# TensorE's filler products before the first group: from full 32-bit products of 128 columns to one-pass products of 128, 256 and 512 columns

## The chip, the cores and the metric

The kernel runs on one core of a Trainium2 chip. The metric is device time in microseconds (us), the median of several runs. Its engines are TensorE (PE, with its weight loads, PEld), VectorE (DVE), ScalarE (ACT), GpSimd (POOL) and SyncE (SP, which here only issues transfers). Each runs its own list of instructions in order and waits for the others by semaphores. TensorE's clock is granted by a throttle, and the profile records it.

## The reference

A gated linear recurrence over 768 steps for 4 batches and 8 heads of 48 channels is followed by a layer with a cosine gate. Cut to what is computed:

```
a_n = a * min(|a|, 0.999) / (|a| + 1e-6)          # a = a_re + i a_im
for t in range(768):
    S = a_n[t] * S + outer(k[t], v[t])            # complex state, 48 x 48 per head
    y[t] = q[t] @ real(S)
x = y as (3072, 384)
h = x @ w_in                                      # (3072, 2048)
out = (h * cos(h)) @ w_out                        # (3072, 384)
```

## The kernel before

The 3072 rows are cut into 24 chunks of 128 steps, taken two at a time: 12 groups. For a group the kernel computes logarithms of the gates' magnitudes and their angles, sums both along time by products with triangular matrices, scales and turns keys and queries by the results, and then needs only matrix products: scores within a chunk, a state carried between chunks, and the two products of the layer.

The function concerned is `fast_path`. For the first group the order on each engine is written out by hand (lines 1225 to 1247); afterwards a helper, `weave`, spreads steps over each other by given shares. All of TensorE's work passes through `matmul` (line 683) or through the transposes of `f_turn` and `f_columns` (lines 918 and 976), each chained behind the one before it, so TensorE's order is that of the program. Since the helper records them, most TensorE instructions of the profile carry line 684, and VectorE's and ScalarE's carry 673, 699 (table load) or 703 (functions from a table): they are told apart by their tiles.

The steps of the first group that the text speaks of, in TensorE's order:

- `busy(12)` at line 1227: twelve filler products whose result is read by no one. The stationary operand is the identity `ident`, the moving one the triangular matrix `sums[0]`. Both are constants that ScalarE's queue fetches at the start (lines 572 and 573), `ident` first.
- `p_powers(0, i)` for the two chunks (line 1232): a product `lgs` of `sums[0]` with the logarithms `lg`, 384 columns; ScalarE takes two exponentials of it (`lg`, here also named `P`, and `Q`). After each, `busy(8)`.
- `g_angle`: ScalarE's arctangent over both chunks into `tan`. Then `g_phase` for each chunk: products `phs` of `turns` with `tan`, and for the second chunk a product of `last` with the first chunk's result; ScalarE rounds `phs`, VectorE subtracts.
- `g_trig`, `p_apply`, `g_stack`: sines and cosines, and the products that make the turned keys `ks` and queries `qs`. Ahead of `g_stack`, `busy(12)`.
- then `f_turn` (tile `tp`, transposes of `ks` and `qs` into `kT` and `qT`), `f_scores` (`sc`), `f_state` (`sp`), `f_rows` (`yr`), `f_columns` (`xp`) of both chunks, and the first group's layer (`hp`).

Fillers write to a buffer of the same PSUM rotation of five (`pa`, tag "a") as `lgs`, `phs`, `tp`, `sc` and the others. From the third group on, the phases and the sums of logarithms are products in the one-pass form of 32-bit floats, with an upper and a lower half of the operand (`hi`, `lo`, line 784). Weights arrive as 64-bit floats in the tile `raw` by GpSimd's queue and are put together by VectorE and ScalarE into `w_in` and `w_out` (line 619).

Of the kernel before, what the change touches and what calls it, by code (L numbers as in the profile page):

```python
# [11 lines left out]
F32 = mybir.dt.float32  # L12
# [3 lines left out]
F32R = mybir.dt.float32r  # L16
# [471 lines left out]
def fast_path(ctx, tc, q, k, v, a_re, a_im, moe_w_in, moe_w_out, out, least, odd, wide):  # L488
# [6 lines left out]
    nc = tc.nc  # L495
    B, H, S, D = q.shape
    DM, DF = moe_w_in.shape
    C = 128
# [21 lines left out]
    stage = {"pool": room.enter_context(tc.tile_pool(name="stage", bufs=1)), "bufs": 4}  # L520
    pa = ctx.enter_context(tc.tile_pool(name="pa", bufs=5, space=PSUM))
# [11 lines left out]
    def constant(array, name, queue=nc.scalar, pool=consts):  # L533
        t = pool.tile(list(array.shape), F32, name=name)
        queue.dma_start(out=t, in_=nc.inline_tensor(array, name=name + "_const").ap())
        return t

    def scalar_tile(value, name):
        t = consts.tile([C, 1], F32, name=name)
        nc.vector.memset(t, value)  # L540
        return t
# [30 lines left out]
    ident = constant(np.eye(C, dtype=np.float32), "ident", pool=stage["pool"])  # L572
    sums = [constant(sums_np[0], "sums", pool=stage["pool"])]
# [61 lines left out]
                          accum_out=odd[:, ds(next(odds), 1)])  # L635

    nc.vector.memset(odd, 0.0)
    odds = iter(range(odd.shape[1]))
    carrier_b = scalar_tile(2.0 ** 23, "carrier_b")
    least_e_b = scalar_tile(897.0, "least_e_b")  # L640
# [8 lines left out]
    def chain(ins, engine="scalar"):  # L649

        if engine in tail:
            behind(ins, tail[engine])
        tail[engine] = ins
# [29 lines left out]
    def matmul(out, **kw):  # L683
        chain(nc.tensor.matmul(out, **kw), "tensor")  # L684

    def busy(count):

        ps = pa.tile([C, C], F32, tag="a", name="busy")
        for _ in range(count):
            matmul(ps, lhsT=ident, rhs=sums[0], start=True, stop=True)  # L690

    tables = {AF.Ln: "natural_log_exp_and_others", AF.Exp: "natural_log_exp_and_others",
              AF.Arctan: "trig_and_small", AF.Sin: "trig_and_small"}
# [2 lines left out]
    def preload(table):  # L696
        if loaded[0] != table:
            loaded[0] = table
            chain(nc.scalar.preload_act_table_set(table))  # L699
# [87 lines left out]
    def p_powers(g, i):  # L787

        x = X[g]
        if i == 0:  # L790
            x["P"], x["Q"] = x["lg"], temp("Q")
            x["row"] = rows_d.tile([G * DM], F32, tag="row", name="row")
            x["end"] = ft.tile([D2, G * H], F32, tag="end", name="end")
        ps = pa.tile([C, DM], F32, tag="a", name="lgs")
        summed_up(ps, g, i, "lg", sums[0])
        special(out=cut(x["P"], i, 1), in_=ps, func=AF.Exp)
        special(out=cut(x["Q"], i, 1), in_=ps, func=AF.Exp, scale=-1.0)
# [68 lines left out]
    def g_trig(g, i, n):  # L866
        x = X[g]
        if i == 0:
            x["cos"] = temp("rs")
            if g:  # L870
                x["sin"] = temp("lg")
        cs, sn = cut(x["cos"], i, n), cut(x["sin"], i, n)
        ph = cut(x["tan"], i, n)
        vector.tensor_scalar(out=cs.bitcast(U32), in0=ph.bitcast(U32),
                                scalar1=0x7FFFFFFF, scalar2=None, op0=ALU.bitwise_and)
        special(out=sn, in_=ph, func=AF.Sin, scale=TWO_PI)
        special(out=cs, in_=cs, func=AF.Sin, scale=-TWO_PI, bias=half_pi_b)

    def g_stack(g, i, n):
        x = X[g]  # L880
        if i == 0:
            for name in "ks", "qs":
                x[name] = gt.tile([C, G * H, 2, D], F32, tag=name, name=name)
        for name, product in ("ks", "Q"), ("qs", "mag"):
            for a, trig in enumerate(("cos", "sin")):
                vector.tensor_tensor(
                    out=x[name][:, ds(i * H, n * H), a],
                    in0=cut(x[product], i, n).rearrange("p (x d) -> p x d", d=D),
                    in1=cut(x[trig], i, n).rearrange("p (x d) -> p x d", d=D), op=ALU.mult)
# [334 lines left out]
    chain(nc.gpsimd.tensor_copy(out=exact, in_=ones), "gpsimd")  # L1224
    Ordered.by_hand = True
    preload("natural_log_exp_and_others")
    busy(12)
    one, two = (log_steps(0, i, 1) for i in range(2))
    for _ in range(5):
        next(one), next(two)  # L1230
    for i in range(2):
        p_powers(0, i)
        busy(8)
    next(one), next(two)
    g_angle(0, 0, 2)
    for i in range(2):
# [3 lines left out]
    g_trig(0, 0, 1)  # L1240
    p_apply(0, 0, 1)
    g_trig(0, 1, 1)
    busy(12)
    g_stack(0, 0, 1)
    p_apply(0, 1, 1)
    g_stack(0, 1, 1)
# [32 lines left out]
def kernel(ctx, tc, q, k, v, a_re, a_im, moe_w_in, moe_w_out, out):  # L1279
# [9 lines left out]
    odd = keep.tile([C, moe_w_in.shape[0] // C * 4 + NJ + NG + 1], F32, name="odd")  # L1289
    wide = keep.tile([C, NG * NJ // 2], F32, name="wide")  # L1290
    late = fast_path(tc, q, k, v, a_re, a_im, moe_w_in, moe_w_out, out, least, odd, wide)
    low = keep.tile([D2, 1], F32, name="low")
    nc.vector.tensor_reduce(out=low, in_=least, axis=AX.X, op=ALU.min)
# [58 lines left out]
```

## Time and profile before

| what | value |
|---|---|
| time, median of 3 runs | 676.51 us (676.01 to 678.98) |
| span of the profiled execution (no other time is given for it) | 677.3 us |
| TensorE busy / weight loads busy | 647.8 us / 580.3 us |
| VectorE / ScalarE busy | 490.3 us / 396.4 us |
| instructions | 10771 |
| mean granted TensorE clock | 0.985 |
| filler instructions on TensorE | 80 (two for each of 40 products), with 80 weight loads |

In the views, a row of instructions reads: start, duration, engine, line, operation, the written tile and the read ones, the shape of the stationary operand, the shape of the moving one, their number, and in brackets the idle time before them and what ended it. A row of stages reads: the stretch, its length, busy time and instructions of PE, PEld, DVE, ACT and POOL, the granted clock as a share of full speed, the share of the DMA engines, and GB/s.

### The profile page before, as it was taken

The numbers are of one execution on the slowest core, as the hardware profiler recorded it, in microseconds if no ns is written. First come the engines' busy times: TensorE is split into PE (matmuls) and PEld (weight loads), VectorE is DVE, ScalarE is ACT, GpSimd is POOL, SyncE is SP. The second block draws the span as 40 slices with busy tenths as digits, with TensorE's granted clock in tenths as the row PEclk, the third lists the DMA queues.
The fourth block names the chain that finished last, engine by engine and source line by source line (L and its number), as shares of the span: only waits on it lengthen the run. The fifth ranks groups of instructions, "written<-read, shape, count | busy, mean of one in ns | idle before, by whom it ended". The sixth has DMA issues, their size and how long they took to land.

```text
span 677.3 us, 10771 instructions
## 1 busy us (share of the span) xinstructions
PE 647.8 (96%) x4080; PEld 580.3 (86%) x4080; DVE 490.3 (72%) x792; ACT 396.4 (59%) x730; POOL 28.5 (4%) x47
## 2 busy tenths in 40 slices
PE   5788889999999999999999999999999999999995
PEld 5686657886799999999999999989999989999895
DVE  4879888759868778868768778868768769762251
ACT  5869775475466467367467467467367467432330
POOL 2011100000000000000000000000000000000000
PEclk8979899999999999999999999999999999999998
DMA  9778623923743864764864864854864753363000
GB/s 244 176 234 224 173 72 81 227 66 69 213 92 63 219 137 116 210 142 109 224 140 118 210 140 113 214 113 126 223 145 118 211 138 78 116 139 116 24 6 24
DMA packets 232810, 94.90 MB, mean 140 GB/s; under 512 B 208798, under 2 KB 221217, under 8 KB 232748
## 3 DMA queue, kind: packets, MB, share of 16 engines
q1 hardware_dynamic: 226252, 68.62, 44.5%
q0 software_dynamic: 5632, 25.17, 11.4%
q8 instruction: 34, 0.56, 0.4%
q10 hardware_dynamic: 864, 0.33, 0.2%
q14 instruction: 28, 0.23, 0.1%
HBM read 69.28 MB, written 24.81 MB: 139 GB/s over the span
## 4 chain that ended last, share of the span: by engine, by line
PE 79%; DVE 6%; DMA 6%; ACT 5%; issue 2%; SPq 1%; DVEq 0%; ACTq 0%
PE hp L684 32%; PE sum L684 15%; PE op L684 14%; PE yp L684 5%; PE sc L684 5%; PE sp L684 3%; PE phs L684 2%; DVE w_in L673 1%; PE lgs L684 1%; DMA raw<-in_moe_w_out_dram 1%; DMA xT<-x 1%; DMA qT<-moved 1%; DVE mag L673 1%; PE yr L684 1%; ACT L699 1%
## 5 line engine op out<-in xcount | busy, mean ns | idle before, releaser
L684 PE MATMUL hp<-xT,w_in 128*128 128x256 f32 x1152 | 254.2, 382 | 1.3 <-ACT xT L673 0.6
L684 PEld LDWEIGHTS hp<-xT,w_in 128*128 128x128 f32 x1152 | 219.9, 192 | 34.6 <-DMA xT<-x 1.9
L703 ACT ACTIVATE gate<-hp,half_pi_b 128x512 f32<-128x512 f32 x96 | 65.9, 686 | 128.0 <-PE hp L684 128.0
L673 DVE TENSOR_TENSOR gate<-hp,gate 128x512 f32<-128x512 f32 x96 | 65.5, 683 | 58.4 <-ACT junk L673 58.4
L684 PE MATMUL op<-w_out,gate 128*128 128x192 f32 (+1 forms) x448 | 103.0, 375 | 2.7 <-DVE w_out L673 2.7
L684 PEld LDWEIGHTS op<-w_out,gate 128*128 128x128 f32 x448 | 75.7, 190 | 19.7 <-DVE w_out L673 3.9
L673 ACT ACTIVATE junk<-hp 128x512 bf16<-128x512 f32 x96 | 56.5, 588 | 0.0
L684 PE MATMUL sum<-t_s,s 128*128 128x192 f32 x320 | 55.3, 326 | 0.0
L684 PEld LDWEIGHTS sum<-t_s,s 128*128 128x128 f32 x320 | 52.6, 190 | 0.0
L673 DVE TENSOR_TENSOR atm<-sc,causal 128x512 f32<-128x512 f32 x48 | 33.0, 687 | 25.4 <-PE sc L684 25.2
L684 PEld LDWEIGHTS sc<-qT,kT 96*128 96x128 f32 x384 | 47.6, 192 | 4.2 <-issue 2.2
L684 PE MATMUL sc<-qT,kT 96*128 96x128 f32 x384 | 49.4, 276 | 1.9 <-ACT qT L673 0.9
L673 ACT ACTIVATE ot<-sum 128x192 f32<-128x192 f32 x30 | 9.5, 320 | 49.4 <-PE sum L684 49.4
L699 ACT ACT_TABLE_LOAD x26 | 33.4, 1283 | 4.0 <-DMA ident<-ident_const 3.6
L673 ACT CAST tan<-phs 128x384 int32<-128x384 f32 x24 | 11.5, 479 | 39.7 <-PE phs L684 39.7
L673 DVE SCALAR_TENSOR_TENSOR ot<-op,ot 128x192 f32<-128x192 f32 x31 | 11.0, 354 | 32.3 <-ACT ot L673 23.5
L684 PE MATMUL yp<-atm,v 128*48 128x128 f32 x352 | 33.5, 277 | 0.0
L684 PEld LDWEIGHTS sp<-v,ks 128*96 128x96 f32 x320 | 29.7, 165 | 0.0
L684 PE MATMUL sp<-v,ks 128*96 128x48 f32 x320 | 29.6, 245 | 0.0
L684 PE MATMUL sum<-w_out,gate 128*128 128x192 f32 x160 | 29.6, 329 | 0.0
L684 PE MATMUL yp<-qT,state 96*48 96x128 f32 x304 | 29.6, 272 | 0.0
L684 PE MATMUL op<-t_a,gate 128*128 128x192 f32 x160 | 29.0, 332 | 0.0
(137 smaller groups left out, 992.7 us busy)
## 6 DMA issues: line engine op xcount, KB each, us to landing
moved<-tr SPq DMA_DIRECT2D x20, 768.0 KB
raw<-in_moe_w_in_dram POOLq DMA_DIRECT2D x16, 768.0 KB, 5.5
raw<-in_moe_w_out_dram POOLq DMA_DIRECT2D x16, 768.0 KB, 4.9
kT<-moved SPq DMA_DIRECT2D x40, 192.0 KB
qT<-moved SPq DMA_DIRECT2D x10, 768.0 KB
k<-in_k_dram SPq DMA_DIRECT2D x24, 192.0 KB
q<-in_q_dram SPq DMA_DIRECT2D x24, 192.0 KB
v<-in_v_dram SPq DMA_DIRECT2D x24, 192.0 KB
```

The lines of the kernel that those rows point to most:

```text
L673: ins = getattr(self.engine, op)(**kw)
L684: chain(nc.tensor.matmul(out, **kw), "tensor")
L699: chain(nc.scalar.preload_act_table_set(table))
L703: chain(nc.scalar.activation(func=func, **kw))
```

## The change

A new tile `idle`, 128 x 512 of 32-bit floats, is filled with ones by VectorE at the start. The fillers read it in place of `sums[0]`, with a given number of moving columns, and both operands are read in the one-pass form of 32-bit floats (`F32R`). The counts change: 12 of 128 columns become 20 of 256; 8 of 128 become 10 of 512 after the first `lgs` and 16 of 128 after the second; 12 of 128 become 24 of 256 ahead of `g_stack`.

```diff
@@ -635,6 +635,8 @@
     nc.vector.memset(odd, 0.0)
+    idle = stage["pool"].tile([C, 512], F32, name="idle")
+    nc.vector.memset(idle, 1.0)
     odds = iter(range(odd.shape[1]))
@@ -683,11 +685,12 @@
-    def busy(count):
+    def busy(count, width):
 
-        ps = pa.tile([C, C], F32, tag="a", name="busy")
+        ps = pa.tile([C, width], F32, tag="a", name="busy")
         for _ in range(count):
-            matmul(ps, lhsT=ident, rhs=sums[0], start=True, stop=True)
+            matmul(ps, lhsT=ident.bitcast(F32R), rhs=idle[:, 0:width].bitcast(F32R),
+                   start=True, stop=True)
@@ -1224,13 +1227,13 @@
     preload("natural_log_exp_and_others")
-    busy(12)
+    busy(20, 256)
     one, two = (log_steps(0, i, 1) for i in range(2))
     for _ in range(5):
         next(one), next(two)
     for i in range(2):
         p_powers(0, i)
-        busy(8)
+        busy((10, 16)[i], (512, 128)[i])
     next(one), next(two)
     g_angle(0, 0, 2)
@@ -1240,7 +1243,7 @@
     g_trig(0, 1, 1)
-    busy(12)
+    busy(24, 256)
     g_stack(0, 0, 1)
```

## The prediction

> **What bounds the kernel now.** I read the page first, then the instructions of TensorE over the first 75 us, then the chain of waits there, then busy time by stage with the granted clock, and last the one-pass products that the kernel already has. The page gives the whole:
>
> ```profile
> PE 647.8 (96%) x4080; PEld 580.3 (86%) x4080; DVE 490.3 (72%) x792; ACT 396.4 (59%) x730; POOL 28.5 (4%) x47
> PE   5788889999999999999999999999999999999995
> PEclk8979899999999999999999999999999999999998
> PE 79%; DVE 6%; DMA 6%; ACT 5%; issue 2%; SPq 1%; DVEq 0%; ACTq 0%
> ```
>
> TensorE sets the end: it is full from about 120 us, and nothing of the change lies there. All fillers run before 26 us, in slices where TensorE is not full. So the change counts only by how it moves the first group's chain, whose delay later work then inherits. TensorE's instructions in order of time (start, duration, tiles; times overlap by the pipeline's depth):
>
> ```profile
> 4.12 4.81 PE L684 MATMUL busy<-sums,ident 128*128 128x128 f32 x24 [4.12 <-DMA sums<-sums_const]
> 12.10 1.65 PE L684 MATMUL lgs<-lg,sums 128*128 128x384 f32 x2 [3.16 <-DVE lg L673]
> 13.54 2.61 PE L684 MATMUL busy<-sums,ident 128*128 128x128 f32 x16
> 15.99 0.81 PE L684 MATMUL lgs<-lg,sums 128*128 128x384 f32 x2
> 16.63 1.95 PE L684 MATMUL busy<-sums,ident 128*128 128x128 f32 x16
> 19.91 1.56 PE L684 MATMUL phs<-tan,turns 128*128 128x384 f32 x4 [1.33 <-ACT tan L703]
> ...
> 22.74 2.84 PE L684 MATMUL busy<-sums,ident 128*128 128x128 f32 x24
> 26.56 1.08 PE L918 MATMUL tp<-ident,ks 128*96 128x128 f32 x8 [0.98 <-DVE ks L673]
> ```
>
> Blocks one, three and four end before an idle stretch: 3.16 us before lgs, 1.33 before phs, 0.98 before tp. Block two has none behind it. The second lgs starts the moment it is through, though its input was written by VectorE at 13.52 (12.96 + 0.56). The chain of waits agrees:
>
> ```profile
> 12.10 1.65 PE lgs L684 x2
> 13.75 2.40 PE busy L684 x16
> 16.15 0.66 PE lgs L684 x2
> ...
> 16.83 0.49 ACT lg L703
> 17.32 0.38 ACT Q L703
> ...
> 17.72 1.28 ACT L699
> ...
> 19.02 0.85 ACT tan L703
> ```
>
> The clock, by stages (us, busy per engine, granted clock, DMA):
>
> ```profile
> 11.50:12.00 0.50, 0.00 (x0) 0.00 (x0) 0.50 (x1) 0.47 (x2) 0.00 (x0) 0.51 1.09 378
> 12.00:14.50 2.50, 2.40 (x7) 1.79 (x8) 1.55 (x4) 2.47 (x6) 0.00 (x0) 0.50 1.06 322
> 14.50:15.00 0.50, 0.50 (x5) 0.50 (x5) 0.47 (x2) 0.15 (x1) 0.00 (x0) 0.58 0.92 343
> 15.00:18.50 3.50, 3.50 (x29) 3.12 (x27) 3.40 (x8) 1.65 (x3) 0.00 (x0) 1.00 1.05 384
> ```
>
> The 0.58 of 14.5 to 15.0 puts the return to full speed at 14.92. Later half-speed stretches are 42.2 to 52.5 and 69.5 to 72.9.
>
> [...]half speed lasts 3.41 us here (11.51 to 14.92) and three times that at 42.2. [...]a 32-bit product is two instructions, each some 0.107 us for 128 columns at full speed. The one-pass spacing comes from this trace:
>
> ```profile
> L684 PE MATMUL phs<-hi,exact x20: 336/404/633, 118.2 to 579.6; 128*128 128x384 f32 x20
> L684 PE MATMUL phs<-lo,exact x20: 336/337/343, 118.7 to 580.0; 128*128 128x384 f32 x20
> ```
>
> At 118.85, 119.03, 119.20 and 119.37 one such product of 384 columns starts each 0.173 us, against 0.33 for each of the two instructions of the plain form (15.99 to 16.63 for two). One pass is thus one instruction at half the column time.
>
> **The change part by part.** Per filler, at full speed: 512 columns, 0.173 + 128/384 of 0.16 = 0.226 us; 256 columns, some 0.12; 128 columns between 0.06 (columns alone) and 0.115 (the spacing of thin products that load 128 weights: yr, 1.95 us for 16). An old instruction takes 0.113. Half speed doubles the column part.
>
> Block one, 24 old instructions to 20 of 256 columns: 2.7 to 2.4 us at full speed, 5.1 to 4.3 at half. It no longer waits for sums (4.12) but for ident, issued 0.4 us ahead of it, and for the fill of idle. It should start between 2.8 and 3.7, and end between 6 and 8 instead of 8.9. Its cover is the wait for lg at 12.10, so it costs nothing. The fill of 128x512 on VectorE isn't in the trace: from 0.06 (the small fills) to 0.69 us (a 128x512 product), taken 0.4, hidden because VectorE next works at 5.83. Without that cover it would delay the first lg by its own length.
>
> Block two, 16 old instructions to 10 of 512 columns, is on the path. Full speed: 10 x 0.226 = 2.26 against 16 x 0.113 = 1.81, +0.45. Half speed: 4.3 against 3.4, +0.87. With the clock as recorded: from 13.54 to 14.92 some 3.2 fillers at 0.43, the other 6.8 at 0.226 make 1.54, so the second lgs starts at 16.46 instead of 15.99: +0.47. Behind it on TensorE are lgs and phs; ScalarE waits to take lg and Q from lgs, then changes its table and does the arctangent. That arctangent can't go ahead before VectorE's last tan (16.83), far too early to hide the delay.
>
> Block three, 16 instructions of 128 columns: 1.0 to 1.84 us against 1.84. Started at 17.1, it ends at 19.0 at the latest, and phs then starts at 20.4: nothing. Block four, 24 of 256 columns: 24 x 0.12 = 2.9 against 2.7. The idle 0.98 us covers 0.2, and both its start and ks move by the same 0.47: nothing.
>
> PSUM: a filler tile grows to one buffer of the same rotation of five, no new wait. SBUF: 2 KB a partition. No DMA is added or moved, on no queue. Sum: +0.47 at tp. From there to 120 us the chain is of turns, copies, table loads and transfers that are issued as VectorE and ScalarE free their buffers, so I let it through whole: 677.3 + 0.5 = 677.8 for the profiled execution. Its span (no other time is given for it) lies 0.8 above the median 676.5, within the three runs (676.0 to 679.0). With up to +1.1 where the earlier end of block one leaves the first lgs at half speed that now has full (2 x 0.32 = 0.64 us), I take +0.6: **677.1**, own range 676.8 to 677.7.
>
> **The rivals.**
> A. *The clock's grid decides.* [...]At 42.2 to 46.4 yr runs at half speed and is on the chain: full speed there would save about 1.9, and 0.4 on xp. Another window at half speed in 27 to 40, where TensorE is over 90% busy, costs up to 1.7. For it: the three runs differ by 3 us. Against a bias: it may fall either way. One saved stretch gives 677.1 - 2.3 = 674.8; upward I take the slowest run before plus 0.6, 679.6. Two stretches at once could pass the bounds below.
> B. *Slower: one-pass products don't count as activity.* [...]the clock stays at half. Block two takes 4.3 from 13.5 to 17.8 (+1.8), the second lgs +0.64, three pairs of phs on the chain +1.3, block four 5.1 us from 26 (tp +0.5 over its own delay), then 16 turns at +0.107 (+1.7) until the clock returns: about +6, **682.5**. [...]Against it: no stage of this trace has one-pass products in number, so nothing here shows it[...].
> C. *The one-pass reading isn't made,* and each filler becomes two instructions of four passes in all: block two 20 x 0.45 = 9 us, block four 48 x 0.22 = 10.6: about +14, 690. Against it: the hi and lo products show one record each (60 for 20 phases of three on average).
> D. *A gain:* the clock is still full at 12.10. Then the first lgs saves 0.64 and block two takes 2.26 instead of 2.45: 675.7.[...]
>
> **How the numbers follow.** The main case 0.62. A 0.22, of it 0.03 beyond either bound of 0.5% (3.4 us, about what a measurement of this kernel can tell from no change). B 0.09, C 0.02, D 0.05. Slower by over 0.5%: 0.03 + 0.09 + 0.02 = 0.14. Faster: 0.03. Within: 0.62 + 0.16 + 0.05 = 0.83. The range takes the main case, D and most of A, and leaves out B and C: 674.8 to 679.6.
>
> **What would show it.** Right: fillers with one instruction per product; block one starting before 4; block two about 2.9 to 3.0 us from 13.5, second lgs near 16.4, tp near 27.0; nothing else moved before it[...]. Wrong: half speed lasting through block two or after 25 (B), two records per filler (C), first lgs in under 1.2 us (D), or half-speed windows elsewhere than 42 to 52 and 70 to 73, which outweigh the +0.5 (A). Were phs to start at 19.9 still, block two is not on the path and the step is wrong.

## The result

The changed kernel takes 680.69 us (median of 7 runs, 679.75 to 681.99) against 678.39 for the kernel before, measured beside it (675.48 to 679.14): a ratio of 1.0048 with a 95% interval of 1.0028 to 1.0068. A repetition with more runs gave 1.0033 (1.0018 to 1.0048). The change costs some 2 to 3 us: within the 0.5% that the chances spoke of, but outside the range of the prediction, and nearly four times its +0.6. One thing about the scale: the three runs known beforehand had a median of 676.5, while the kernel before, over the 282 runs that accompany the experiments, has a mean of 679.0 and a standard deviation of 1.5. About 2 us of the distance from 677.1 to 680.7 is that scale; the rest is the matter of this study.

The page of the changed kernel, its span, the busy time, the clock and the chain:

```profile
span 678.9 us, 10753 instructions
PE 649.5 (96%) x4070; PEld 580.4 (85%) x4070; DVE 490.1 (72%) x793; ACT 396.7 (58%) x730; POOL 27.7 (4%) x47
PEclk9979899999999999999999999999999999999999
PE 76%; DMA 9%; ACT 7%; DVE 5%; issue 2%; SPq 0%; ACTq 0%; DVEq 0%
```

The span is 1.6 us longer, TensorE does ten instruction pairs fewer, and the share of DMA in the chain has gone from 6 to 9%. That last number is the one the prediction has nothing to say on. TensorE's instructions of the first group in the changed kernel (start, duration, tiles):

```profile
2.69 4.61 PE L686 MATMUL busy<-idle,ident 128*128 128x256 f32 x20 [2.69 <-DMA ident<-ident_const]
12.11 1.65 PE L686 MATMUL lgs<-lg,sums 128*128 128x384 f32 x2 [4.82 <-DVE lg L675]
12.98 3.95 PE L686 MATMUL busy<-idle,ident 128*128 128x512 f32 x10
16.77 0.81 PE L686 MATMUL lgs<-lg,sums 128*128 128x384 f32 x2
20.70 1.56 PE L686 MATMUL phs<-tan,turns 128*128 128x384 f32 x4 [1.38 <-ACT tan L706]
27.25 1.08 PE L921 MATMUL tp<-ident,ks 128*96 128x128 f32 x8 [0.69 <-DVE ks L675]
```

Here the reader sees the predicted part: one instruction per product, block one starting at 2.7, block two from the first lgs to the second, which starts 0.78 us later than before (16.77 against 15.99); tp follows 0.69 later. But the two traces, laid beside each other further on, don't keep this distance. By ScalarE's table loads the changed kernel is 0.8 us *ahead* at 200 to 312 us: TensorE waited 2.69 us instead of 3.96 ahead of the second group's phs at 65 to 69, which was not followed further. It is level at 351 to 401, behind by 1.34 at 414, and by 2.0 at 566. So in this pair the loss arises after 315 us, in a stretch whose instructions are the same in both kernels.

### The profile page after: what moved, and what is told of

It reads as the page before. It is cut to its first block, busy times and chain, and to the rows that moved or that the text cites. A ratio compares the mean times of both kernels' runs of the same rounds, so it can differ in the third digit from the quotient of the medians.

```text
span 678.9 us, 10753 instructions
## 1 busy us (share of the span) xinstructions
PE 649.5 (96%) x4070; PEld 580.4 (85%) x4070; DVE 490.1 (72%) x793; ACT 396.7 (58%) x730; POOL 27.7 (4%) x47
## 4 chain that ended last, share of the span: by engine, by line
PE 76%; DMA 9%; ACT 7%; DVE 5%; issue 2%; SPq 0%; ACTq 0%; DVEq 0%
PE hp L686 34%; PE op L686 13%; PE sum L686 12%; PE yp L686 4%; PE sc L686 4%; DMA raw<-in_moe_w_out_dram 4%; PE sp L686 3%; PE phs L686 2%; DMA xT<-x 2%; PE lgs L686 1%; DMA x<-yT 1%; DVE w_in L675 1%; DMA qT<-moved 1%; DVE lg L675 1%; ACT L702 1%
```

## The late stall

In this pair of traces one wait is new, at 396 us. In the waits of TensorE between 380 and 410 us the kernel before has none; the changed kernel has:

```profile
PE sc L686 <- DMA qT<-moved: 1.3, 1, 1.3
```

The scores wait for the queries' transfer. SyncE's queue, in the kernel before:

```profile
386.75 5.26 SPq L906 DMA_DIRECT2D kT<-moved  x4
392.12 1.29 SPq L908 DMA_DIRECT2D qT<-moved  x1
```

and in the changed kernel:

```profile
386.49 6.41 SPq L909 DMA_DIRECT2D kT<-moved  x4
393.00 0.92 SPq L911 DMA_DIRECT2D qT<-moved  x1
```

The four transfers of the keys were asked for at the same time, but their issue took 1.15 us longer, and the queries' went out 0.9 later. What the DMA engines did meanwhile, in the changed kernel, by stages of 1 us (the last two columns are the share of the DMA engines and GB/s):

```profile
390.50:391.50 1.00, 1.00 (x6) 0.88 (x5) 0.96 (x3) 0.57 (x1) 0.00 (x0) 1.00 0.90 136
391.50:392.50 1.00, 1.00 (x7) 0.87 (x6) 0.81 (x3) 0.70 (x3) 0.00 (x0) 1.00 0.09 14
392.50:393.50 1.00, 1.00 (x6) 0.90 (x5) 0.42 (x1) 0.00 (x0) 0.00 (x0) 1.00 0.77 122
```

For about a microsecond the engines are 9% busy, in the middle of a transfer that TensorE will wait for; in the kernel before the stage from 391.5 shows a share of 0.82 and 129 GB/s. The queues of the changed kernel from 387 to 394 us name a guest:

```profile
q8 instruction: 1, 0.02, 0.8%
```

A packet of 16 KB of queue 8 started at 389.89 and took 0.95 us, so it was over some 0.6 us before the gap; in the kernel before that packet started at 386.34, ahead of the keys' transfer. The queue's kind is `instruction`, and an execution has 34 packets on it in either kernel, 16 KB each. The trace doesn't say whose instructions they are. TensorE shows 8160 matmuls and weight loads, 240 to a packet; the page counts 1569 for VectorE, ScalarE and GpSimd together; so the packets are taken here for TensorE's. Twenty instructions fewer (ten matmuls, ten weight loads) are a twelfth of a packet, and the packets are 19.8 us apart in the median: from this a packet would come 1.7 us later, as an estimate. In this pair the 34 came between 0.9 us earlier and 6.1 us later than in the kernel before, 1.9 later in the median, and the one at 386 us 3.55 later. The hypothesis: it now falls among the pieces of 128 bytes in which kT is moved (of the 4786 packets from 387 to 394 us 4673 are of under 512 bytes), and the issue of the rest is held up. How a packet would do that, the traces don't show.

The kernel before is not free of such long issues, though: only its first profile is. In its second one (the run against itself, below) two other groups have them:

```profile
285.11 6.31 SPq L906 DMA_DIRECT2D kT<-moved  x4
539.53 6.33 SPq L906 DMA_DIRECT2D kT<-moved  x4
```

Packets came at 289.9 and 544.0, near the end of these issues; the DMA share was 0.10 from 291 to 292 us; and TensorE waited 0.7 and 1.2 us before the scores. A new stall in one pair of traces is thus no measure of the change: what counts is how often they come, and what they add up to, over all profiles. The experiments had to tell this from the delay of block two and from the clock.

## The experiments

Each was timed beside runs of the kernel before. Blocks one to four are the fillers ahead of the first lgs, between the two, ahead of phs and ahead of g_stack. Unless said otherwise the edits are to lines of the hand-written order.

**The kernel before against itself.** No edit.

> The kernel before, once more, against itself: the size of what two runs of one program can differ by, and a second profile of it. Every theory expects a ratio of 1.000 within 0.003. If its profile falls among the faster executions of before (675.5 to 676.5 us) rather than the slower (678.4 to 679.1), it shows what sets the two apart; the theory of the clock's grid expects a missing half-speed stretch between 42 and 52 us, worth 2 to 4 us.

Measured: 1.000 (0.9980 to 1.0010). The profiled execution was at 679.8, with half-speed stretches at 11.7 to 15.1, 42.4 to 52.7 and 69.7 to 73.1 as in the first profile but 0.2 us later. In the first profile the clock changed at 11.51, 14.92, 42.23, 52.47, 69.54 and 72.95, always a whole multiple of 3.41 us apart, and in the changed kernel at 42.81, 53.05, 70.12 and 73.53 with the same spacing, 0.58 us later: that is the grid. In the profiles of the other kernels it falls differently each time (full speed came back at 16.24, 17.65 and 17.79 in three of them). Over the 57 runs of the kernel before that go with it the time goes with the mean granted clock: those at 0.982 and 0.983 have means of 681.4 and 680.9 us, those at 0.987 and 0.988 of 678.2 and 676.6. One kernel's executions thus spread by some 4 us along with the clock, which a different place of the grid would explain; no run sets that place, so it isn't shown as the cause. A profile without the stretch at 42 to 52 was not seen.

**The tile alone.** The tile of ones is allocated and filled in the kernel before, and not read.

> The kernel before with the tile of ones allocated and filled but read by nobody, all fillers as before. The theory that the filler blocks make the delay expects no change (678 us, ratio 1.000 within 0.003). The theory that the tile's 2 KB a partition shift other tiles' addresses and slow transfers or reads later expects most of the 3.3 us (ratio 1.003 to 1.006).

Measured: 0.9990 (0.9976 to 1.0005). The place in memory is not the cause.

**Block two alone.**

```diff
-        busy(8)
+        one_pass(10, 512) if i == 0 else busy(8)
```

> The kernel before with the tile of ones and block two alone as changed: ten one-pass products of 512 columns; the other blocks as before. The theory of the path (block two delays the second lgs) expects the second lgs near 16.7 instead of 15.99 and tp 0.5 to 0.8 us later, and at the end +0.5 to +1.1 us if the delay is passed on whole (ratio 1.0007 to 1.0016), up to the measured +3.3 if it grows on the way. The theory that block one decides, by ending at 7.3 us and leaving the clock at half speed, expects at most +0.9.

Measured: 1.0034 (1.0022 to 1.0047), 681.85 us: as much as the whole change in its repetition. The second lgs started at 17.83, at half speed of the clock throughout (it returned at 17.65), tp at 28.31, 1.75 later than in the first profile of before, and the stall at 396 was there too, with an issue of kT of 6.44 us. This kernel has 74 filler matmuls, 6 fewer than before: it carries both suspects, and does not tell them apart.

**All but block two.**

```diff
-        busy((10, 16)[i], (512, 128)[i])
+        two_pass(8) if i == 0 else busy(16, 128)
```

> The changed kernel with block two alone put back: eight two-pass products of 128 columns; blocks one, three and four as changed. The theory of the path expects tp within 0.2 us of before and no change at the end (ratio 1.000 within 0.002). The theory that block one decides expects +2 to +3 us (ratio 1.003 to 1.005), with the first lgs at half speed and the clock back later than in before.

Measured: 1.0009 (0.9989 to 1.0028), 680.46 us. Inconclusive: its profile fell on a grid with an additional half-speed stretch at 21.0 to 24.4, and its 76 fillers again shift the packets (issue of kT 6.48 us at 388.9).

**Fewer instructions and nothing else.** Block one of the kernel before from 12 products of 128 columns to 7 of 300.

```diff
-    busy(12)
+    two_pass(7, 300)
```

> The kernel before with 10 instruction pairs fewer on TensorE and nothing else to its path: block one is 7 two-pass products of 300 columns over the tile of ones (14 matmuls, ending between 7.6 and 9.3 us) in place of 12 of 128 (24 matmuls). Theory of the fetch: [...]with 20 instructions fewer every packet comes some 2 to 4 us later against the work, and in the groups after 386 us it falls among the 128-byte transfers of kT and qT, as in the three slower kernels. It expects nothing at tp, the stall of 1.0 to 1.5 us at 396 us, and +1.5 to +2.5 us at the end (ratio 1.002 to 1.004). Theory of the path alone: no change (ratio 1.000 within 0.002).

Measured: 1.0010 (0.9993 to 1.0028). In the trace the stall appears as foreseen: kT's issue takes 6.45 us, the packet of instructions at 390.8 lies within it, scores wait 1.1 us for qT. The median is too uncertain to call, so this run alone doesn't show that fewer instructions cost anything; its runs also have the highest mean clock but one of all the kernels (0.9869 against 0.9851).

**The columns split over twice the instructions.** Block two of 20 products of 256 columns, 80 fillers as before.

```diff
-        busy((10, 16)[i], (512, 128)[i])
+        busy((20, 16)[i], (256, 128)[i])
```

> The changed kernel with block two as 20 products of 256 columns in place of 10 of 512: the same columns, 10 instruction pairs more, so that TensorE has as many as before. Both theories expect the early delay (second lgs near 16.8, tp +0.7). Theory of the fetch: the packets fall where they did before, no new stall at 396, and only +0.8 to +1.3 us at the end (ratio 1.001 to 1.002). Theory that the early delay itself grows: +3 us as in the changed kernel (1.0045).

Measured: 1.0019 (1.0004 to 1.0035). Early delay as in the changed kernel (second lgs at 17.38), no stall at 396, issue of kT 5.03 us; but a long one of 6.30 us at 540, with a wait of 1.0 us behind it.

**Block two narrower.** Ten products of 400 columns, 70 fillers.

```diff
-        busy((10, 16)[i], (512, 128)[i])
+        busy((10, 16)[i], (400, 128)[i])
```

> The changed kernel with block two of 10 products of 400 columns: as many instructions as in the changed kernel, but as much column time as before[...]. The early delay goes (second lgs near 16.0, tp within 0.2). Theory of the fetch: the stall at 396 and those after it stay, +1.5 to +2.5 us (ratio 1.002 to 1.004). Theory that the early delay is all: 0 (ratio 1.000 within 0.002).

Measured: 1.0032 (1.0016 to 1.0049): by the spacings in the traces (0.235 us for 512 columns, 0.112 for an old instruction) 1.84 us at full speed against 1.79 before, an estimate, and yet the loss of the changed kernel. kT's issue 6.36 us, scores wait 0.6 us for qT at 396. The early delay was less clearly gone than expected: the second lgs came at 16.54 and tp at 27.02, with the clock back at 16.24.

**Block two put back and the number restored.** As all but block two, with block three of 20 products.

> The changed kernel with block two put back (8 two-pass products) and block three of 20 products instead of 16, hidden before phs: neither the early delay nor fewer instructions than before. Theory of the fetch with the path: no change (ratio 1.000 within 0.002), no stall at 396. If block one's earlier end matters by itself, +0.6 to +2 us remain, with the first lgs at half speed and the clock back later.

Measured: 1.0019 (1.0005 to 1.0034), where the theory had 1.000 within 0.002. In the trace the issue of kT at 386 takes 5.22 us and the scores wait 0.4 us at 396; but the issue at 540 takes 6.73 us, with a wait of 1.3 us behind it. The second lgs is at 16.06. The mean clock of its runs is among the lowest, 0.9834 against 0.9851, which at the 0.5 us per 0.001 that a fit to the runs of the kernel before gives would be some 0.9 us of its 1.3 in the mean. Whether block one or block four is behind it, this run can't tell.

**The changed kernel again.** No edit to it.

> The changed kernel once more, for a narrower interval and a second profile of it. Every theory expects a ratio of 1.003 to 1.0055, the second lgs between 16.4 and 18.0 by the place of the clock's grid, and the instruction packet near 390 us among the transfers of kT, with the stall of about 1 us after it.

Measured: 1.0033 (1.0018 to 1.0048), 681.19 us. Second lgs at 17.71 with the clock back at 17.79, packet at 391.9, issue of kT 6.36 us.

**Block one alone, number kept.** The kernel before with block one as changed and block three of 10 products.

```diff
-    busy(12)
+    one_pass(20, 256)
...
-        busy(8)
+        busy((8, 10)[i])
```

> The kernel before with block one alone as changed (20 one-pass products of 256 columns, over by 7.4 us instead of 8.9), and block three of 10 two-pass products instead of 8, hidden before phs, so that TensorE has as many instructions as before. Theory of the earlier end: the clock is less often at full speed in 8 to 16 us, the mean clock is lower by 0.001 to 0.002 than before, +0.4 to +0.9 us (ratio 1.0005 to 1.0015), no new stall at 396. If block one is covered, as the prediction had it: ratio 1.000 within 0.001.

Measured: 1.0001 (0.9986 to 1.0017). Block one's earlier end costs nothing that can be measured, which agrees with the prediction that it is covered. The interval still takes in the +0.4 to +0.9 us of the theory of the earlier end, so that is made unlikely and not refuted.

**Block one of the old length in the changed kernel.** 30 products instead of 20, so 80 fillers.

```diff
-    busy(20, 256)
+    busy(30, 256)
```

> The changed kernel with block one of 30 products of 256 columns instead of 20: it lasts about as long as before the change (to between 8 and 9.2 us), and TensorE has as many instructions as before. Of the three parts that the theory names (block two's delay, the earlier end of block one, the packets) only the first is left: +0.5 to +1.3 us (ratio 1.0007 to 1.002), no new stall at 396. If something else in the change costs, it stays at 1.004 or more.

Measured: 1.0014 (1.0000 to 1.0028); no stall at 396, issue of kT 5.21 us, second lgs at 17.76. What is left with the number restored is what the delay of block two was expected to leave. (Its runs have the lowest mean clock of all, 0.9832.)

**Block two moved away.** The kernel before, nothing between the two lgs.

```diff
-    busy(12)
+    busy(16)
...
-        busy(8)
+        if i == 1:
+            busy(12)
```

> The kernel before with block two taken out from between the two lgs: blocks one and three take its products (16 and 12), so the number of instructions stays. Theory of the path, from its other side: the second lgs starts near 13.6 instead of 15.99, the arctangent waits for VectorE's last tan at 16.8 instead of for TensorE and runs near 17 instead of 19.0, tp 1.0 to 2.0 us earlier; -1.0 to -2.0 us at the end (ratio 0.997 to 0.9985). If block two is not on the path: no change. The clock may take some of it back, if the block after the second lgs is at half speed and reaches into phs.

Measured: 0.9969 (0.9956 to 0.9983), 677.27 us: faster than both kernels. TensorE in its first group:

```profile
12.30 0.91 PE L684 MATMUL lgs<-lg,sums 128*128 128x384 f32 x2 [2.85 <-DVE lg L673]
13.77 1.28 PE L684 MATMUL lgs<-lg,sums 128*128 128x384 f32 x2 [0.56 <-DVE lg L673]
14.85 4.16 PE L684 MATMUL busy<-sums,ident 128*128 128x128 f32 x24
18.84 1.46 PE L684 MATMUL phs<-tan,turns 128*128 128x384 f32 x4
```

The second lgs now waits for VectorE (0.56), not for fillers, and phs starts 1.07 us earlier than in the kernel before; it would be more if block three didn't reach to 18.8. The path argument holds from both sides in the traces. In the time the clock may have a share: the runs of this kernel have the highest mean clock, 0.9870 against 0.9851.

Two runs then changed the number alone, against the changed kernel, in block three, which is hidden before phs:

```diff
-        busy((10, 16)[i], (512, 128)[i])
+        busy((10, 26)[i], (512, 128)[i])
```

> The changed kernel with block three of 26 products of 128 columns instead of 16, hidden before phs: blocks one, two and four and the early delay as in the changed kernel, but as many instructions on TensorE as before. Theory of the fetch: no long issue of kT at 386 and no new stall at 396; about 1 us less than the changed kernel, +1.0 to +1.6 us over before (ratio 1.0015 to 1.0024). If the number of instructions doesn't matter: 1.0033 to 1.0048, as the changed kernel.

Measured: 1.0024 (1.0010 to 1.0039). SyncE's queue:

```profile
387.61 5.05 SPq L909 DMA_DIRECT2D kT<-moved  x4
392.77 1.26 SPq L911 DMA_DIRECT2D qT<-moved  x1
```

The issue is as short as before, the packet came at 387.1 ahead of it, and TensorE has no wait at 396, though the second lgs (17.59) is as late as in the changed kernel. The group of 540 has the long issue instead (6.37 us). In the mean this kernel is 1.0 us faster than the changed one, about as much as the two can differ by chance.

```diff
-        busy((10, 16)[i], (512, 128)[i])
+        busy((10, 6)[i], (512, 340)[i])
```

> The changed kernel with block three of 6 products of 340 columns instead of 16 of 128 (as many columns): ten instruction pairs fewer again. Theory of the fetch: each packet comes 2 to 4 us later than in the changed kernel, at about 393 us for the group of 386, at the end of kT's issue and among qT's transfers; the stall at 396 changes in size or goes to another group, and the end stays +1.5 to +3 us over before (ratio 1.002 to 1.0045). If the number doesn't matter: the stall of 396 stays as in the changed kernel, about 1 us with the issue of kT at 6.4 us.

Measured: 0.9992 (0.9975 to 1.0008): the expectation of +1.5 to +3 us was wrong in sign. With ten pairs fewer again the changed kernel is as fast as the one before, with its early delay still there (second lgs at 17.13). SyncE's queue in two groups:

```profile
235.44 6.41 SPq L909 DMA_DIRECT2D kT<-moved  x4
...
389.60 4.65 SPq L909 DMA_DIRECT2D kT<-moved  x4
394.36 1.92 SPq L911 DMA_DIRECT2D qT<-moved  x1
```

At 386 the packet (394.2, against 389.9 and 391.9 with 70 fillers and 387.1 with 80) comes only at the end of the keys. The long issue went to the group of 235, with a packet at 238.8 inside it and a step of 0.95 us at 244. The steps of 1.24 and 0.42 us that this profile lacks at 474 and 483, against the second profile of the changed kernel, were not followed to their cause. The number of TensorE's instructions thus moves the time, and not in proportion: 80, 70 and 60 fillers gave 1.0024, 1.0033 and 0.9992 with the same blocks on the path. The step from 70 to 60, 2.4 us in the mean, is clear of the noise; that from 80 to 70 barely.

**Both parts turned round.** The kernel before with no filler between the two lgs and 6 products behind the second; block one of 22 products (80 fillers), or of 12 as before (60).

```diff
-        busy(8)
+        if i == 1:
+            busy(6)
```

> The kernel before without block two, its products moved to block one (22 products instead of 12) and block three cut to 6 so that it is over before the arctangent; as many instructions as before. Theory of path and packets: the second lgs near 13.7, phs near 18 instead of 19.9, tp about 2 us earlier, packets as before: -1.7 to -2.6 us (ratio 0.996 to 0.9975). If the path were only block two's own delay: no more than the -2.1 that moving it gave.

> As the kernel without block two and with block three of 6 products, but with block one of 12 as before: 60 filler matmuls, 20 fewer than before. Theory of path and packets: the number that took the changed kernel from +2.2 to -0.1 us (60 against 70) should give no less than the number of before: -1.5 to -3.5 us (ratio 0.995 to 0.998). If the number doesn't matter: as the kernel with 80, less what the longer block one gives the clock.

Measured: 0.9980 (0.9964 to 0.9997) with 80, 0.9965 (0.9951 to 0.9978) with 60, 676.68 us. The first lies above its expected 0.996 to 0.9975 but with phs at 17.62 as foreseen; the second is within its own, though its profile fell on half speed from 12.9 to 23.1 us and has phs at 18.35 and tp at 26.38. The number's own part between these two, some 0.6 us in the mean, is within their intervals. The version with 60 is the fastest of all here, by a margin over the one with block two moved that isn't resolved.

**The sum.** Twelve kernels make a table of three choices: block two's columns (5120, or some 4000; those of an old instruction count twice, since at full speed it takes 0.112 us for 128, and a product of 512 takes 0.235), at least 4 filler matmuls fewer than before, and block one ending early. A least-squares fit to all their runs (left out are those with 60 fillers and those without block two) gives +1.1 us (± 0.4) for block two, +1.1 (± 0.4) for the smaller number, +0.3 (± 0.3) for block one. They add up to 2.5; the changed kernel's 29 runs have a mean of +2.2 over the kernel before. Block four was never changed alone. Taken into the fit as a fourth choice, it gets +0.5 (± 0.6) and block one 0.0, and the other two keep +0.9 and +1.1: a cost of block four is neither shown nor excluded.

The fit shares out an average over executions. How the smaller number acts, the traces show only in part. Of the ten profiles with 80 fillers none has a long issue of kT at 386 us, but six have one at 540 and two at 285 (5.9 to 6.7 us). Of the six with 70 to 76 fillers all have one at 386 (6.4 to 6.5 us), and one has one at 540. Fewer fillers thus move the long issue more than they add one. Added up from 120 to 640 us, TensorE's waits at the scores come to 1.1 us in the mean of the profiles with 80 fillers, 1.6 with 70 to 76, and 0.75 in the two with 60. With one profile for each kernel these are few, but the order is that of the times; the size, 0.5 us, is about half of the +1.1 of the fit. Where the other half arises is open.

## Why the prediction was wrong

The step that failed is the sentence "No DMA is added or moved, on no queue." The kernel's own transfers weren't, but the 34 packets of queue 8 are transfers too, and the number of TensorE's instructions, whose packets they are taken for, changed by 20; the one at 386 us came 3.55 us later. The part list counted how long 80 and 70 filler instructions take and not what it means that there are 10 fewer: the number entered the sum at nothing. The page before had the line of queue 8 with its 34 packets and 0.56 MB, 16 KB each. By the fit the smaller number came to +1.1 us on average; that the number moves the time is shown by 70 against 60 fillers; that it does so by the place of the packets is the author's reading of few profiles, and covers about half of it (0.5 us of waits at the scores). The rest of the miss is a term of the sum: block two's delay, taken at +0.47 and with its margin at +0.6, came to +1.1 by the same fit.

The starting point was low as well. The prediction set the span of the traced execution, 677.3, against times. In all runs that have both on record the time lies 1.7 to 1.9 us above the span, so the traced execution was the one of 678.98, the slowest of the three, and the median of 676.5 lay 2.5 below the later mean. From that mean, +0.6 gives 679.6 and the measured +2.2 gives 681.2: it takes the low start and the missed terms together to set 677.1 so far from 680.7.

By its other steps:

- *Block two is on the path, +0.47.* Right in mechanism and sign, low in size. The profile before happened to have the clock back at 14.92, in the middle of the block. In seven profiles with the wide block two the second lgs started at 16.77 to 17.83, where seven with the old block two (the first profile of before among them) had 15.99 to 17.02; the means are 17.45 and 16.40. The price was right where the clock is alike: put back at 15.50, as in the profile of the changed kernel (its record of the clock begins there, at full speed, and its products of 512 columns start 0.43 us apart up to 15.26 and 0.235 from 15.62), the prediction's own sum gives 16.73 for its second lgs, which came at 16.77. With half speed through the whole block it came at 17.71, 17.76 and 17.83, against 17.00 and 17.02 with the old block: +0.76, within the +0.45 to +0.87 that were worked out. The remainder of the 1.05 between the means is the place of the clock, which gave full speed back at 16.3 us or later in six of the seven wide profiles and in two of the others; whether by chance or by the change isn't shown. The +1.1 stood for another case, a first lgs that loses full speed; in both profiles of each kernel it had half speed (1.65 us).
- *Passed on whole to 120 us and the end.* In the mean about right: +1.1 at the end for +1.0 at the second lgs. In a single pair of traces it isn't: the 0.8 us were gained back and more by 69 us and lost again after 315.
- *Blocks one, three and four cost nothing.* Block one, tried alone: 1.0001, within 1 us. Three and four end before phs and tp in all the profiles of the changed kernel (idle 1.38 us behind the one, 0.69 and 0.71 behind the other); neither was tried alone.
- *Rival A, the clock's grid.* Executions of one kernel do spread by 4 us along with the clock. It isn't the difference: the 22 runs of the changed kernel in its repetition have a mean clock of 0.9851, as have the 75 of the kernel before beside them.
- *Rival B, the clock stays at half behind one-pass products:* refuted. In the second profile of the changed kernel the clock rose at 7.55; block one ran from 2.68 to 7.28, so TensorE had done nothing but one-pass fillers up to then.
- *Rival C:* refuted, 70 records for 70 products. *Rival D:* the first lgs was at half speed in the changed kernel's profiles (1.65 us).

## What to carry to other kernels

A filler delays its successor on the engine wherever that was ready earlier (the second lgs of the kernel before had its input at 13.52 and started at 15.99): fillers belong in front of a wait for another engine, and here two products whose inputs come 1.5 us apart left no room between them. When instructions are added to or taken from an engine with thousands of them, the packets of the instruction queue can move against the work (here, with 20 of 8160 fewer, by -0.9 to 6.1 us); compare versions with the number held constant, or try a few numbers, before a difference of some tenths of a per cent is put down to what the instructions do. And where executions of one kernel differ by 4 us, three runs give no baseline for a forecast of 1 us.

## What the hardware showed

- With a single 16 KB packet of the instruction queue, 0.95 us long, in the middle of transfers in pieces of 128 bytes (at 389.89 in the changed kernel, 3.4 us after the start of their issue at 386.49), the DMA engines fell to a share of 0.09 for about 1 us. The issue of four transfers on SyncE's queue took 6.36 to 6.48 us there in all six profiles with 70 to 76 fillers instead of 5.03 to 5.41, and TensorE waited 0.6 to 1.5 us before the scores. With the packet 0.4 to 0.5 us ahead of the issue (386.34 against 386.75 in the kernel before, 387.1 against 387.61 with block three of 26) the issue took 5.26 and 5.05 us, and none of the ten profiles with 80 fillers has a long one there. Near the end of the issue it goes either way in the kernel before: with the packet at 544.19 the issue from 539.33 took 4.94 us, with the packet at 544.0 that from 539.53 took 6.33.
- The clock rose behind one-pass products alone: at 7.55 in the second profile of the changed kernel, 0.27 us after a block one of nothing else. In the first profile the same block, 4.6 us long, was not followed by full speed (all its 20 products at half speed, 0.213 us apart), and the clock came back only at 15.50. What decides between the two was not shown.
- One-pass products of 128 columns start 0.112 us apart at full speed in block three, no closer than the instructions of the old fillers and of yr with its 48 columns (0.112 each). What the three have in common is a load of 128 weights each (0.19 us in the median); whether that sets the spacing was not shown.
